# Query products as fp32 in two column halves, and a new order, in the attention stage of a gated mix

## The chip, the cores and the metric

The kernel runs on one core of a Trainium2 chip. The metric is the time of one execution on the device in microseconds (us); smaller is better. Beside the times there is a trace of one profiled execution, in which TensorE is called PE, VectorE DVE, ScalarE ACT, GpSimd POOL and SyncE SP.

## The reference

For one sequence of S = 2048 tokens with D = 576 features, the result is a mix of a linear attention and a gated MLP, by a gate of its own for each token:

```python
g = sigmoid((x * gate_w).sum(-1, keepdims=True))
# a: 32 heads of 18 features
pq, pk = q @ w_phi, k @ w_phi                         # per head
phi_q = concat([softmax(pq), softmax(-pq)])           # 36 features a head
phi_k = concat([softmax(pk), softmax(-pk)])
kv, z = phi_k^T @ v, phi_k.sum over tokens            # per head: 36 x 18, 36
a = ((phi_q @ kv) / (phi_q @ z + 1e-6)) @ wo
b = (max(x @ W_gate, 0) * (x @ W_up)) @ W_down        # F = 4608
return g * a + (1 - g) * b
```

## The kernel before

Everything is fp32. Most products are made on PE in fp32r, with every operand split into a high part (a rounded copy, made by ACT) and a low part (the difference, made by DVE), so that one product is three matmuls: high by high, high by low, low by high. Some small products and all transposes take fp32 operands as they are.

The work falls into three stages.

**Projections and state.** Token tiles of 128 are projected into keys, values and queries (`project`, L179). `key_steps` (L268) and `query_steps` (L344) make the two softmaxes of a tile on DVE, ACT and POOL. `kv_step` (L408) adds a tile into the state: eleven fp32 matmuls, one for each group of 54 value columns with its ones column, the odd groups into rows 64 and up of the same PSUM bank, the even ones into the rows from 0. `turn` (L365) transposes the query features of a tile, in three parts (`QN`: groups 0 to 3, 4 to 7, 8 to 10), to [108 features, 11 groups, 128 tokens]. Tiles before `FIRST` = 12 are stored in DRAM (`eT`); the last four are split right away into operands `phh`, `phl` (L374). The last steps of this stage (L585 on) are written out by hand, with an order for PE kept by `in_order`; the other engines are ordered by a scheduler.

**Attention output.** The state is transposed (`kv_turn`) and masked into per-group weights `kvm` (`kv_blocks`, L505), split into `kvh` and `kvl`. The tokens are then handled in four blocks of 512, in the order 3, 0, 1, 2 (`BLOCKS`). For each block:

- `sums` (L531): for each of six row tiles (`ORDER` = 4, 5, 3, 2, 1, 0) two groups are multiplied into one PSUM bank, three fp32r matmuls for a group, 108 rows deep and 114 columns wide: 108 numerators and six denominators. That is 33 matmuls a block.
- `sums_out` (L540): ACT evicts the 114 rows into `R[:, i]` or a tile `og`; SP copies the denominator rows into a tile `dn` of [128, 128] by a small DMA, and POOL's queue fills the rows 108 to 127 of `R` from row tile 4 (L550) and the fifth row tile from row tiles 4 and 5 (L553, L554).
- `invert` (L689): DVE takes the reciprocal of `dn`, multiplies by the gates, which stand transposed in `gT`, spreads them over four masked copies (`rd`, 128x512) with `cmask`, and the result is split (`rdh`, `rdl`).
- `divide` (L705): for each of the five row tiles two matmuls by `spread` bring the inverted denominators to the rows of `R`; DVE multiplies, ACT and DVE split into `oh` and `ol`.
- `project_out` (L732) and `rows_out` (L756): the output projection by `wo`, 65 matmuls a block, goes over k (the row tile of the input) and for each k over five PSUM banks, one for each row tile m of the output; the five are evicted at the end and stored in `att` in DRAM.

For blocks 0, 1 and 2 of the sequence the query features come back from `eT` in `fetch` (L424) and are split by `prepare_high` and `prepare_low` (L433, L438). `out_weights` (L442) splits `wo` early and stores it in DRAM; `load_out_weights` (L675) loads it back before the output stage. The order of PE in this stage (L915 to L1034) works out as: the sums of the next block between the divisions of the one before, the projection of a block behind the sums of the block after it. `operand_ahead`, `in_place`, `unit` and `load_w` between them are preparations of the third stage.

**Main loop.** The MLP goes over 72 units of 7 products (`step`, L1315), each of 7 matmuls, with the down products between; the attention is added from `att`, in tiles `ac`. Here the order of all engines is fixed by `in_order` (L1473).

Of the kernel before, what the change touches and what calls it, by code (L numbers as in the profile page):

```python
# [15 lines left out]
P = 128  # L16
# [10 lines left out]
NJ = -(-H // HG)  # L27
QH = 3
QG = QH * DH
QK = 2 * QG  # L30
QM = G + 2 * QH
# [51 lines left out]
def gated_mix_kernel(  # L83
# [14 lines left out]
    cmask_d: bass.AP,  # L98
# [15 lines left out]
    keep = ctx.enter_context(tc.tile_pool(name="keep", bufs=1))  # L114
    dram = ctx.enter_context(tc.tile_pool(name="dram", bufs=1, space=bass.MemoryType.DRAM))
# [8 lines left out]
    wohd = dram.tile([P, 5, 5, P], F32, name="wohd")  # L124
    wold = dram.tile([P, 4, 5, P], F32, name="wold")
    sprd = dram.tile([P, 5, P], F32, name="sprd")
# [4 lines left out]
    A, A2, AR = ExitStack(), ExitStack(), ExitStack()  # L131
# [7 lines left out]
    raw = AR.enter_context(tc.tile_pool(name="raw", bufs=4))  # L139
# [108 lines left out]
    pp = A.enter_context(tc.tile_pool(name="pp", bufs=2, space=PSUM, reuse_waits="tile"))  # L248
    pv1 = A.enter_context(tc.tile_pool(name="pv1", bufs=1, space=PSUM, reuse_waits="tile"))
# [53 lines left out]
    def half_gates(hf):  # L303

        c = slice(hf * NT // 2, (hf + 1) * NT // 2)
        nc.vector.tensor_scalar_add(gs[:, c], gs[:, c], 1.0)
        nc.vector.reciprocal(gs[:, c], gs[:, c])
        nc.vector.tensor_scalar(out=ng[:, c], in0=gs[:, c], scalar1=-1.0, scalar2=1.0, op0=MULT, op1=ADD)
# [8 lines left out]
    def on_all_rows(ps, dst, tb):  # L317

        for i in range(4):
            t = 4 * tb + i  # L320
            nc.tensor.transpose(ps[:, i * P:(i + 1) * P], rs[:, t:t + 1].to_broadcast([P, P]), ident)
        nc.scalar.activation(dst, ps, AF.Copy)
# [42 lines left out]
    def turn(t, b, ps=None):  # L365
# [36 lines left out]
    ps_kv = A.enter_context(tc.tile_pool(name="ps_kv", bufs=1, space=PSUM, reuse_waits="tile"))  # L402
# [16 lines left out]
    def operands(tb):  # L419
        PH[tb] = [[ph.tile([QK, len(n), TB], F32R, name=f"ph{a}{n.start}") for a in "hl"] for n in QN]  # L420

    ER = {}

    def fetch(t):  # L424
        ER[t] = er.tile([QK, NQ, P], F32, name="er")
        nc.sync.dma_start(ER[t].rearrange("p g t -> p (g t)"), eT[t * QK:(t + 1) * QK])

    def part(tb, i, p):
        if tb not in PH:
            operands(tb)  # L430
        return *(a[:, :, i * P:(i + 1) * P] for a in PH[tb][p]), ER[4 * tb + i][:, QN[p].start:QN[p].stop]

    def prepare_high(tb, i, p):  # L433

        h, l, r = part(tb, i, p)
        nc.scalar.activation(h, r, AF.Copy)

    def prepare_low(tb, i, p):  # L438
        h, l, r = part(tb, i, p)
        tt(out=l, in0=r, in1=h.bitcast(F32), op=SUB)  # L440

    def out_weights(m):  # L442

        w = raw.tile([P, 5, P], F32, name="wor", tag="raw")
        nc.sync.dma_start(w, wo[m] if m < 5 else spread_d)
        o = raw.tile([P, 2, 5, P], F32R, name="woo", tag="raw")
        nc.scalar.activation(o[:, 0], w, AF.Copy)
        if m < 4:
            tt(out=o[:, 1], in0=w, in1=o[:, 0].bitcast(F32), op=SUB)
            nc.sync.dma_start(wold[:, m], o[:, 1].bitcast(F32))  # L450
        elif m == 4:
            tt(out=o[:, 0, :, 64:], in0=w[:, :, 64:], in1=o[:, 0, :, 64:].bitcast(F32), op=SUB)
        nc.sync.dma_start(wohd[:, m] if m < 5 else sprd, o[:, 0].bitcast(F32))

    xw = AR.enter_context(tc.tile_pool(name="xw", bufs=4, **R_))
    first_half = iter(())
    for t in range(2, NT - 2):
# [10 lines left out]
        if t == 12:  # L468
# [6 lines left out]
            ph = RS.enter_context(tc.tile_pool(name="ph", bufs=1, **R_))  # L475
            kt = kt_p.tile([P, NJ, QK], F32, name="kt")
            gsx = kt_p.tile([P, NTB, H, 4], F32, name="gsx")
            operands(BLOCKS[0])
        keys(t)
# [10 lines left out]
        if t in (2, 3, 4, 5, 7, 8):  # L490
            out_weights((2, 3, 4, 5, 7, 8).index(t))
# [13 lines left out]
    def kv_blocks(q):  # L505

        n, ps = min(4, NQ - 4 * q), PKV[q]
        for p in range(2):
            gs_ = slice(4 * q + p, 4 * q + n, 2)
            ng = len(range(p, n, 2))  # L510
            r = 64 * p
            if q == 2 and p == 0:
                tt(out=kvm[:, 8, 0:QG], in0=ps[:, 0, 1:1 + QG], in1=mask, op=MULT)
                tt(out=kvm[:, 10, DH:QG], in0=ps[:, 1, 1:1 + QG - DH], in1=mask[:, DH:], op=MULT)
            else:
                tt(out=kvm[:, gs_, p * QG:(p + 1) * QG], in0=ps[:, 0:ng, r + 1:r + 1 + QG],
                   in1=mask[:, None, :].to_broadcast([QK, ng, QG]), op=MULT)
            nc.vector.scalar_tensor_tensor(
                out=kvm[:, gs_, G + 3 * p:G + 3 * p + 3], in0=ps[:, 0:ng, r:r + 1].to_broadcast([QK, ng, 3]),
                scalar=eps, in1=hm[:, None, :].to_broadcast([QK, ng, 3]), op0=ADD, op1=MULT)  # L520
        nc.scalar.activation(kvh[:, 4 * q:4 * q + n, :QM], kvm[:, 4 * q:4 * q + n], AF.Copy)

    def kv_low(q):
        n = min(4, NQ - 4 * q)
        tt(out=kvl[:, 4 * q:4 * q + n, :QM], in0=kvm[:, 4 * q:4 * q + n],
           in1=kvh[:, 4 * q:4 * q + n, :QM].bitcast(F32), op=SUB)

    DN, RW, OG, PS = {}, {}, {}, {}
    ORDER = (4, 5, 3, 2, 1, 0)

    def sums(tb, i, ps):  # L531

        PS[tb, i] = ps = ps[:QM]
        parts, pairs = PH[BLOCKS[tb]], []
# [5 lines left out]
    def sums_out(tb, i):  # L540
        if i == ORDER[0]:
            pool = ob if tb % 2 else rb
            DN[tb], RW[tb] = (pool.tile(shape, F32, name=name, bufs=1) for name, shape in (("dn", [P, P]), ("R", [P, 5, TB])))
        dn, R = DN[tb], RW[tb]
        og = OG[i] = R[:QM, i] if i < 4 else rb.tile([P, TB], F32, name="og")[:QM]
        nc.scalar.activation(og, PS.pop((tb, i)), AF.Copy)
        d0, dl = (G, HG) if i < NJ - 1 else (G + 1, 2)
        nc.sync.dma_start(dn[4 * HG * i:4 * (HG * i + dl)], og[d0:d0 + dl])
        if i < 4:
            nc.gpsimd.dma_start(R[G:, i], OG[4][20 * i:20 * i + 20])  # L550
        elif i == 5:
            for r in (0, 64):
                nc.gpsimd.dma_start(R[r:r + 28, 4], OG[4][80:G])  # L553
                nc.gpsimd.dma_start(R[r + 28:r + 64, 4], OG[5][DH:QG])  # L554
# [30 lines left out]
    with in_order(tc, nc, nc.tensor):  # L585
# [3 lines left out]
        run(key_steps, t, (T_(t - 2, 1),), V_(t - 1, 0), F_, K_(t - 2), T_(t - 2, 0))  # L589
        run(query_steps, t, (V_(t - 1, 1),))  # L590
        run(query_steps, FIRST - 2, (V_(t, 0),), V_(t, 1), F_, K_(t - 1), T_(t - 1, 2), K_(t))
        kv_out()
        A2.close()
        kb = RS.enter_context(tc.tile_pool(name="kb", bufs=1, **R_))
        rb = RS.enter_context(tc.tile_pool(name="rb", bufs=2, **R_))
        er = RS.enter_context(tc.tile_pool(name="er", bufs=4, **R_))
        table = kb.tile([QK, 64], F32, name="table")[:, :QG + 4]
# [1028 lines left out]
```

## Time and profile before

| | us |
|---|---|
| median of 3 runs | 1635.37 |
| lowest and highest run | 1634.16, 1635.42 |
| profiled execution | 1633.52 |
| its span in the trace | 1631.7 |
| first state step of the last tile ends, main loop begins on PE | 251.6, 377.9 |

The profiled execution is 1.8 us longer than its span, and 1.9 us below the median of the runs. Its mean granted clock of PE is .991 of full speed. In the profile a line such as "L1204 DVE TENSOR_TENSOR ac<-pd,ac 128x512 f32<-128x512 f32 x238 | 163.9, 689 | 148.0 <-PE pd L1189 147.9" reads: line 1204, on DVE, writes ac from pd and ac, 238 times; 163.9 us busy in all, 689 ns each; DVE stood idle for 148.0 us just before them, 147.9 of it until a product pd of PE at line 1189. L177 is the helper `accumulate`, L371 a transpose in `turn`, L412 the state step and L753 the output projection.

### The profile page before, as it was taken

The numbers are of one execution on the slowest core, as the hardware profiler recorded it, in microseconds if no ns is written. First come the engines' busy times: TensorE is split into PE (matmuls) and PEld (weight loads), VectorE is DVE, ScalarE is ACT, GpSimd is POOL, SyncE is SP. The second block draws the span as 40 slices with busy tenths as digits, with TensorE's granted clock in tenths as the row PEclk, the third lists the DMA queues.
The fourth block names the chain that finished last, engine by engine and source line by source line (L and its number), as shares of the span: only waits on it lengthen the run. The fifth ranks groups of instructions, "written<-read, shape, count | busy, mean of one in ns | idle before, by whom it ended". The sixth has DMA issues, their size and how long they took to land.

```text
span 1631.7 us, 20454 instructions
## 1 busy us (share of the span) xinstructions
PE 1591.5 (98%) x7887; PEld 1341.4 (82%) x7887; DVE 1230.6 (75%) x1907; ACT 579.2 (35%) x960; POOL 181.7 (11%) x266
## 2 busy tenths in 40 slices
PE   9998997998999999999999999999999999999998
PEld 8898996776888888888888887788888888888887
DVE  4998687758777787887777777667777777777777
ACT  4344335655332432332332334232322223222331
POOL 0128212220000000000000002111111111111110
PEclk9999999999999999999999999999999999999999
DMA  8244107466766657556545534553434434343442
GB/s 268 82 158 168 59 17 235 160 216 238 272 222 218 232 197 256 207 194 231 225 171 204 200 123 130 208 198 131 173 138 154 172 130 182 128 177 149 151 160 73
DMA packets 64861, 285.84 MB, mean 175 GB/s; under 512 B 7290, under 2 KB 16890, under 8 KB 55804
## 3 DMA queue, kind: packets, MB, share of 16 engines
q1 hardware_dynamic: 61932, 278.24, 47.1%
q0 software_dynamic: 2256, 5.25, 1.0%
q8 instruction: 62, 1.02, 0.3%
q10 hardware_dynamic: 576, 1.05, 0.2%
q14 instruction: 35, 0.29, 0.1%
HBM read 173.00 MB, written 109.54 MB: 173 GB/s over the span
## 4 chain that ended last, share of the span: by engine, by line
PE 85%; DVE 5%; DMA 4%; ACT 3%; issue 2%; POOL 1%; SPq 0%; POOLq 0%; DVEq 0%; ACTq 0%
PE cx L1126 27%; PE ca L1126 13%; PE pd L1166 12%; PE pd L1189 10%; PE cy L1126 7%; PE kv L177 2%; PE pq L177 2%; PE pm L1166 2%; PE pm L1189 2%; PE pw L753 2%; PE pk L177 2%; PE pv L239 1%; PE po L177 1%; DVE sm L206 1%; PE ptr L371 1%
## 5 line engine op out<-in xcount | busy, mean ns | idle before, releaser
L1233 ACT ACTIVATE hh<-g 128x512 fp32r<-128x512 f32 x195 | 119.9, 624 | 455.0 <-DVE g L1283 285.7
L1204 DVE TENSOR_TENSOR ac<-pd,ac 128x512 f32<-128x512 f32 x238 | 163.9, 689 | 148.0 <-PE pd L1189 147.9
L1126 PE MATMUL cx<-xo,ws 128*128 128x512 f32 x1008 | 253.7, 391 | 4.3 <-ACT g L1287 4.3
L1126 PE MATMUL cx<-xo,wb 128*128 128x512 f32 x1008 | 250.4, 391 | 4.5 <-DVE u L1408 2.7
L1126 PE MATMUL ca<-xo,ws 128*128 128x512 f32 x1008 | 251.9, 389 | 0.0
L1126 PEld LDWEIGHTS cx<-xo,wb 128*128 128x128 f32 x1008 | 188.6, 188 | 46.4 <-DVE u L1408 3.5
L1126 PEld LDWEIGHTS cx<-xo,ws 128*128 128x128 f32 x1008 | 189.9, 189 | 44.8 <-ACT g L1287 5.4
L1126 PEld LDWEIGHTS ca<-xo,ws 128*128 128x128 f32 x1008 | 189.3, 188 | 39.3
L1166 PE MATMUL pd<-hh,wd 128*128 128x512 f32 x576 | 200.7, 389 | 0.0
L1189 PE MATMUL pd<-hh,wd 128*128 128x512 f32 x476 | 185.6, 390 | 0.0
L1172 DVE TENSOR_TENSOR ac<-pd,ac 128x512 f32<-128x512 f32 x144 | 99.1, 688 | 105.9 <-PE pd L1166 103.3
L1238 DVE TENSOR_TENSOR hl<-g,hh 128x512 fp32r<-128x512 f32 x195 | 136.2, 699 | 1.9 <-ACT hh L1233 0.2
L1287 ACT ACTIVATE g<-cx 128x512 f32<-128x512 f32 x144 | 84.7, 588 | 127.4 <-PE cx L1126 127.3
L1166 PEld LDWEIGHTS pd<-hh,wd 128*128 128x128 f32 x576 | 108.1, 188 | 22.5
L1126 PE MATMUL cy<-xo,wb 128*128 128x512 f32 x504 | 126.0, 389 | 0.0
L1089 ACT ACTIVATE wd<-wdr 128x384 fp32r<-128x384 f32 (+1 forms) x106 | 62.3, 606 | 156.5 <-DMA wdr<-wd 156.5
L1166 PE MATMUL pd<-hl,wd 128*128 128x512 f32 x288 | 112.2, 389 | 1.0 <-ACT xo L815 1.0
L1126 PEld LDWEIGHTS cy<-xo,wb 128*128 128x128 f32 x504 | 94.7, 188 | 19.7
L1189 PEld LDWEIGHTS pd<-hh,wd 128*128 128x128 f32 x476 | 89.6, 188 | 18.7
L1189 PE MATMUL pd<-hl,wd 128*128 128x512 f32 x238 | 92.8, 390 | 0.0
L799 POOL TENSOR_TENSOR xo<-xr,xo 32x512 fp32r<-32x512 f32 x5 | 8.2, 1654 | 635.6 <-DVE xo L799 628.0
L1092 DVE TENSOR_TENSOR wd<-wdr,wd 128x384 fp32r<-128x384 f32 (+1 forms) x106 | 69.5, 670 | 6.2 <-ACT wd L1089 6.2
(241 smaller groups left out, 2708.2 us busy)
## 6 DMA issues: line engine op xcount, KB each, us to landing
wsd<-ws SPq DMA_DIRECT2D x34, 1280.0 KB
ws<-wsd SPq DMA_DIRECT2D x34, 1280.0 KB
wbd<-wb SPq DMA_DIRECT2D x34, 960.0 KB
wb<-wbd SPq DMA_DIRECT2D x34, 960.0 KB
wr<-wgu SPq DMA_DIRECT2D x36, 768.0 KB
wdr<-wd SPq DMA_DIRECT2D x36, 576.0 KB
eT<-et SPq DMA_DIRECT2D x12, 594.0 KB
er<-eT SPq DMA_DIRECT2D x12, 594.0 KB
```

What stands on the lines that cost most here:

```text
L177: nc.tensor.matmul(ps, w, m, start=i == 0, stop=i == len(pairs) - 1)
L753: nc.tensor.matmul(ps, w, v, start=len(done) == 1, stop=len(done) == (14 if m < 4 else 9), skip_group_check=True)
L1089: nc.scalar.activation(o[:, 0], a, AF.Copy)
L1092: tt(out=o[:, 1], in0=a, in1=o[:, 0].bitcast(F32), op=SUB)
L1126: nc.tensor.matmul(ps, w, v, start=first and m == 0, stop=m == len(pairs) - 1, skip_group_check=True)
L1166: nc.tensor.matmul(ps, w, v, start=k == 0 and (i < 2 or first), stop=k == len(mms) - 1 and (i < 2 or last), skip_group_check=True)
L1172: tt(out=a, in0=ps, in1=a, op=ADD)
L1189: mm = lambda ps, w, v, a, z: nc.tensor.matmul(ps, w, v, start=a, stop=z, skip_group_check=True)
L1204: tt(out=a, in0=ps, in1=a, op=ADD)
L1233: nc.scalar.activation(h, src, AF.Copy)
L1238: tt(out=l, in0=src, in1=h.bitcast(F32), op=SUB)
L1287: nc.scalar.activation(a, ps, AF.Copy)
```

## The change

1. The products of `sums` take fp32 operands as they are: no `kvh`, `kvl`, `phh`, `phl`. The weights of a group have 64 columns (`QM` = 64): the even group of a row tile goes to PSUM rows 0 to 63, the odd one to 64 to 127. A block has 11 matmuls. `fetch` loads straight into the operand tile; in `turn` one ACT copy stands in place of the split.
2. The denominators of a block are 32 rows of 512 (`dn`), gate rows come by four transposes to 32 columns a block (`rows_of`), and the inverted rows, high over low, are one operand of 64 rows: `divide` has one matmul for a row tile.
3. `project_out` goes over the row tiles m of the output, with all k for one m, in two PSUM banks in turn, and evicts each at once. The split `wo` is loaded from DRAM into the pool `raw` before the last token tiles (at t = 12 of the first loop) and stays there.
4. Blocks: in `project_out(b, m)` stand the sums of block b + 2 and the division of block b + 1. One query tile (10) goes behind the last state step. SP's and POOL's queues follow the program's order too. `fetch` of the third block comes behind the sums of the second.
5. The PSUM pools `pp`, `pv1` and `ps_kv` are kept until the attention is done (`AP`), in place of new pools `pw` and `pb`; `raw` is kept to the end and takes the tiles `ac` of the main loop. `load_w(0)` and what follows it stand behind the last division of block 3, in `project_out(2, 1)`.

The diff, cut to its core:

```diff
+GAP = 10
-QM = G + 2 * QH
+QM = 64
...
-            h, l = (a[:, :, t % 4 * P:(t % 4 + 1) * P] for a in PH[t // 4][b])
-            split(h, l, ps[:, :len(gg)])
+            nc.scalar.activation(PH[t // 4][:, t % 4, gg.start:gg.stop], ps[:, :len(gg)], AF.Copy)
...
+def fetch(tb):
+        operands(tb)
+        for i in range(4):
+            t = 4 * tb + i
+            nc.sync.dma_start(PH[tb][:, i].rearrange("p g t -> p (g t)"), eT[t * QK:(t + 1) * QK])
...
+    def sums(b, i, ps):
+        if i == ORDER[0]:
+            DN[b] = rb.tile([H, TB], F32, name="dn", bufs=1)
+            RW[b] = rb.tile([P, 5, TB], F32, name="R")
+            OG4[b] = rb.tile([P, TB], F32, name="og")
+        dn, R = DN[b], RW[b]
+        n = P if i < NJ - 1 else QM
         for g in range(2 * i, min(2 * i + 2, NQ)):
-            (h, l), o = parts[g // 4], g % 4
-            pairs += [(kvh[:, g, :QM], h[:, o]), (kvh[:, g, :QM], l[:, o]), (kvl[:, g, :QM], h[:, o])]
-        accumulate(ps, pairs)
+            nc.tensor.matmul(ps[g % 2 * 64:g % 2 * 64 + QM], kvm[:, g], PH[BLOCKS[b]][:, :, g], start=True, stop=True)
+        og = (OG4[b] if i == 4 else R[:, i if i < 4 else 4])[:n]
+        nc.scalar.activation(og, ps[:n], AF.Copy)
+        if i < NJ - 1:
+            nc.sync.dma_start(dn[HG * i:HG * i + HG], og[64 - QH:64 + QH])
+        else:
+            nc.sync.dma_start(dn[HG * i:], og[:2])
         if i < 4:
+            nc.gpsimd.dma_start(R[QG:QG + 2 * GAP, i], OG4[b][i // 2 * 74 + i % 2 * 20:][:20])
         elif i == 5:
+            for r, c in ((0, 40), (14, 114)):
+                nc.gpsimd.dma_start(R[r:r + 14, 4], OG4[b][c:c + 14])
...
+    def invert(b):
+        dn = DN.pop(b)
+        ps = kv_bank(0)
+        rows_of(ps, gs, BLOCKS[b], H)
+        nc.vector.reciprocal(dn, dn)
+        tt(out=dn, in0=ps[:H], in1=dn, op=MULT)
+        rd = RD[b] = rb.tile([2 * H, TB], F32R, name="rd", bufs=1)
+        nc.scalar.activation(rd[:H], dn, AF.Copy)
+        tt(out=rd[H:], in0=dn, in1=rd[:H].bitcast(F32), op=SUB)
+
+    def divide(b, k):
+        R = RW[b]
+        n = P if k < 4 else 64
...
+        nc.tensor.matmul(ps[:n], spread[:, k, :n], RD[b], start=True, stop=True)
+        r = R[:n, k]
+        tt(out=r, in0=ps[:n], in1=r, op=MULT)
+        nc.scalar.activation(oh[:n, k], r, AF.Copy)
+        tt(out=ol[:, k] if k < 4 else oh[64:, k], in0=r, in1=oh[:n, k].bitcast(F32), op=SUB)
...
+        last = query_steps(FIRST - 2, middle)
...
+        for i, ps in zip(ORDER, (kv_bank(0), kv_bank(1), two[:, 0], two[:, 1], kv_bank(0), kv_bank(1))):
+            sums(0, i, ps)
...
+        final = query_steps(FIRST - 1, middle)
+        next(final)
+        whole(last)
+        turn(FIRST - 2, 0)
+        turn2(FIRST - 2, 1)
+        turn(FIRST - 2, 2)
+        two = pp.tile([P, 2, TB], F32, name="po", tag="pp")
+        sums(1, ORDER[0], two[:, 0])
+        sums(1, ORDER[1], two[:, 1])
+        next(final)
+        next(final)
+        invert(0)
+        for n in (2, 4):
+            two = pp.tile([P, 2, TB], F32, name="po", tag="pp")
+            divide(0, 6 - n)
+            sums(1, ORDER[n], two[:, 0])
+            divide(0, 5 - n)
+            sums(1, ORDER[n + 1], two[:, 1])
+        fetch(BLOCKS[2])
+        divide(0, 0)
+        whole(final)
+        turn(FIRST - 1, 0)
...
+    def project_out(b, m):
+        ps = kv_bank(2) if m % 2 else pv1.tile([P, TB], F32, name="pw", tag="pv1")
+        oh, ol = OW[b]
+        pairs = []
+        for k in range(4, -1, -1):
+            wh, wl = WOUT[m, k]
+            pairs.append((wh, oh[:, k]))
+            if k < 4:
+                pairs.append((wh, ol[:, k]))
+            if m < 4:
+                pairs.append((wl, oh[:, k]))
+        accumulate(ps, pairs)
...
+        fetch(BLOCKS[3])
+        for b in range(2):
+            for m in range(5):
+                project_out(b, m)
+                if m < 3:
+                    two = pp.tile([P, 2, TB], F32, name="po", tag="pp")
+                    for n in range(2):
+                        sums(b + 2, ORDER[2 * m + n], two[:, n])
+                if m == 0:
+                    invert(b + 1)
+                else:
+                    divide(b + 1, 5 - m)
+                if b == 0 and m in (3, 4):
+                    root_rows(m - 1)
+                if m == 4:
+                    divide(b + 1, 0)
+                    whole((x0, x1)[b])
+        for m in range(5):
+            project_out(2, m)
+            if m == 0:
+                invert(3)
+                divide(3, 4)
+                divide(3, 3)
+            if m == 1:
+                for k in (2, 1, 0):
+                    divide(3, k)
                 RS.close()
...
-    ac = ctx.enter_context(tc.tile_pool(name="ac", bufs=1, **CB))
+    sums_of = [raw.tile([P, 3, TB], F32, name="ac", tag="raw") for _ in range(4)]
```

More of the change, by code (lines that the diff above doesn't have):

```diff
@@ L419, in operands @@
     def operands(tb):
[L420 to L440, printed above, removed]
+        PH[tb] = PP[BLOCKS.index(tb) % 2].tile([QK, 4, NQ, P], F32, name="ph")
+    def fetch(tb):
[3 more added lines that the diff above has]
+            nc.sync.dma_start(PH[tb][:, i].rearrange("p g t -> p (g t)"), eT[t * QK:(t + 1) * QK])
     def out_weights(m):
         w = raw.tile([P, 5, P], F32, name="wor", tag="raw")
-        nc.sync.dma_start(w, wo[m] if m < 5 else spread_d)
+        nc.sync.dma_start(w, wo[m])
         o = raw.tile([P, 2, 5, P], F32R, name="woo", tag="raw")
@@ L540, in sums_out @@
[L540 to L548, printed above, removed]
+                out=kvm[:, gs_, d:d + QH], in0=ps[:, 0:ng, r:r + 1].to_broadcast([QK, ng, QH]),
@@ L647, in gated_mix_kernel @@
-        PH.pop(b0)
-        pg = pp.tile([P, 2, TB], F32, name="pgt", tag="pp")[:, 0]
-        for tb in range(NTB):
-            nc.tensor.transpose(pg[:, tb * P:(tb + 1) * P], gsx[:, tb].rearrange("p h c -> p (h c)"), ident)
-        nc.scalar.activation(gT.rearrange("p b t -> p (b t)"), pg, AF.Copy)
-        turn(FIRST - 1, 0)
-        two = pp.tile([P, 2, TB], F32, name="ptr", tag="pp")[:QK].rearrange("p b (g t) -> p b g t", g=4)
-        turn(FIRST - 1, 1, two[:, 0])
-        turn(FIRST - 1, 2, two[:, 1])
```

375 lines of the change are left out of this document (107 added, 268 removed).

## Prediction

> **What bounds the kernel now.** The page first, then busy time by windows, then the waits of TensorE, then the chain. The page says that TensorE (PE) is the bound as a whole:
>
> ```profile
> span 1631.7 us, 20454 instructions
> PE 1591.5 (98%) x7887; PEld 1341.4 (82%) x7887; DVE 1230.6 (75%) x1907; ACT 579.2 (35%) x960; POOL 181.7 (11%) x266
> er<-eT SPq DMA_DIRECT2D x12, 594.0 KB
> ```
>
> PE is idle for 1631.7 − 1591.5 = 40.2 us in all. The change leaves the order of the main loop alone, so it works only on the attention stage, from about 245 us to the loop's first product at 377.94 us (row below), and on the entry of the loop behind it. What counts is when PE begins unit 0 of the loop; a microsecond there is one at the end, since PE is busy from there on. The windows (length, PE, PEld, DVE, ACT, POOL, granted clock, DMA share, GB/s) show where the stage is not PE's:
>
> ```profile
> 250.00:260.00 10.00, 8.56 (x79) 7.73 (x79) 7.66 (x25) 6.38 (x12) 1.17 (x1) 1.00 0.83 279
> 270.00:280.00 10.00, 6.88 (x36) 4.93 (x34) 7.90 (x13) 6.21 (x13) 3.52 (x7) 1.00 0.78 245
> 280.00:290.00 10.00, 4.11 (x10) 3.15 (x11) 2.54 (x4) 2.99 (x7) 1.38 (x3) 0.56 0.39 129
> 290.00:300.00 10.00, 10.00 (x42) 8.00 (x41) 8.83 (x15) 8.03 (x17) 1.67 (x4) 0.93 0.68 227
> ```
>
> At 280 us PE idles, and afterwards works at about half clock. The waits of PE from 255 to 400 us name the reasons (engine and line that waits, what it waits for, total, times, longest):
>
> ```profile
> PE pd L177 <- ACT og L546: 7.6, 1, 7.6
> PE cx L1126 <- ACT g L1287: 2.7, 1, 2.7
> PE pw L753 <- DVE o L765: 1.8, 1, 1.8
> PE cx L1126 <- DVE u L1408: 1.6, 1, 1.6
> PE ptr L371 <- DVE phl L151: 1.4, 2, 1.1
> PE ptr L371 <- DVE et L382: 1.4, 2, 0.7
> PE ptr L371 <- ACT et L380: 0.7, 1, 0.7
> ```
>
> The chain of waits tells what is behind the 7.6 us, and gives PE's pace in the sums (start, length, what):
>
> ```profile
> 271.42 5.79 DMA dn<-R
> 277.74 7.33 DMA R<-og
> 285.24 0.61 ACT og L546
> 285.89 1.22 PE pd L177 x2
> 312.47 2.77 PE po L177 x12
> 385.02 5.42 DMA wdr<-wd
> ```
>
> ACT could not evict the next og, because a small transfer out of the old og took 7.33 us and had itself waited for a denominator transfer of 5.79 us. So block 0 is bound by small transfers in crowded queues, and everything later by PE.
>
> **The change, part by part.** Sums. Twelve fp32r products take 2.77 us, .231 each, so a block's 33 take 7.6 us. The new block has 11 fp32 products in column halves, which no row shows at 512 columns; the nearest is the state's step L412, eleven fp32 products in the same two halves, 108 columns wide (start, length, engine, line, what):
>
> ```profile
> 249.89 0.54 PE L371 MATMUL ptr<-ident,e 128*108 128x128 f32 x3
> 250.36 1.32 PE L412 MATMUL kv<-e,vt 128*55 128x108 f32 x22
> 251.61 0.40 PE L177 MATMUL pq<-wq_h,xh 128*128 128x288 f32 x1
> 251.85 0.29 PE L177 MATMUL pq<-wq_l,xh 128*128 128x288 f32 x1
> 251.98 0.29 PE L177 MATMUL pq<-wq_h,xl 128*128 128x288 f32 x1
> 253.56 0.60 PE L371 MATMUL ptr<-ident,e 128*108 128x128 f32 x4
> 254.00 0.82 PE L503 MATMUL kv<-ident,kt 128*108 128x128 f32 x6
> ```
>
> ```profile
> 377.94 1.75 PE L1126 MATMUL cx<-xo,wb 128*128 128x512 f32 x7
> ```
>
> Four transposes take 254.00 − 253.56 = .44 us, .11 each. The three ahead of the step take .47, .14 more than .33: entering costs .14. The first product behind it takes .24 and the second .13: leaving costs .11. Together .25 us a visit. Start to start the step takes 1.25 us; less .14 that is 1.11 for eleven products, .101 each. At the pace of the .11 transposes (.86 ns a column and record, two records a product) one alone would take .186, so the halves run beside each other. Widened by 512/108 the block takes 11 × .101 × 4.74 = 5.3 us, or 8.8 to 9.7 if the halves did not overlap. I take 5.3, which is 2.3 less a block and 9.2 in all.
>
> The Trainium skill's page "TensorEngine Tiling (Array Packing)", Key Properties, says that a change of tiling mode drains TensorE, which speaks against this change; by that rule each visit has a price, and the trace agrees with .25 us.
>
> Switches. Sums are visited 12 times (once in block 0, five times in block 1, between divisions, three in each of the others): 3.0 us. Twenty spread products of 64 rows and four sets of 32-column transposes stand between full-size products; no row has these tiles, so 0 to .25 each; I take half, 3.0. Together +6.0, with ends 3.0 and 9.0.
>
> Division. One spread product in place of two: 20 × .231 = −4.6. Gate rows: 16 transposes of 32 columns instead of 4: 12 × .11 = +1.3.
>
> The same page, Gotcha 2, rules out transpose mode for fp32 beside column tiling; by it these transposes might cost two records, 16 × .11 = 1.8 us more. No run here shows it.
>
> Work of PE altogether: −9.2 + 6.0 − 4.6 + 1.3 = −6.5 us.
>
> Stalls that go. The 7.6 us: of og only row tile 4 is left, so its two buffers reach back two blocks instead of one. The 1.4 + 1.4 + .7 at the turns and the 1.8 at L753 (one eviction per row tile, beside the next tile's products) go too: −12.9. The half clock goes as well: the windows grant .56 from 280 to 290 and .93 from 290 to 300 us, so it ends at about 291.4; from 285.9 to there 5.5 us of work took twice its time: −2.7. What is late next is DVE and the queues:
>
> ```profile
> L440 DVE TENSOR_TENSOR phl<-er,phh 108x512 fp32r<-108x512 f32 x24 | 15.6, 682 | 0.3
> L711 DVE TENSOR_TENSOR R<-pd,R 128x512 f32<-128x512 f32 x20 | 13.4, 688 | 16.9 <-PE pd L177 15.1 <-DMA R<-og 1.7
> L726 DVE TENSOR_TENSOR ol<-R,oh 128x512 fp32r<-128x512 f32 x16 | 10.9, 689 | 5.5 <-ACT oh L713 5.1
> L206 DVE TENSOR_REDUCE sm<-e 128x64 f32<-128x1152 f32 x6 | 8.1, 1353 | 3.5 <-ACT e L203 3.5
> L692 DVE RECIPROCAL dn<-dn 128x128 f32<-128x128 f32 x4 | 3.8, 950 | 3.0 <-DMA dn<-R 3.0
> L201 DVE TENSOR_TENSOR e<-pq,mx 128x576 f32<-128x576 f32 x4 | 3.0, 747 | 0.0
> L307 DVE RECIPROCAL gates<-gates 128x8 f32<-128x8 f32 x1 | 0.2, 195 | 0.0
> ```
>
> ```profile
> L713 ACT ACTIVATE oh<-R 128x512 fp32r<-128x512 f32 x20 | 12.2, 627 | 13.4 <-DVE R L711 12.6 <-ACT phh L436 0.8
> L436 ACT ACTIVATE phh<-er 108x512 fp32r<-108x512 f32 x24 | 14.0, 631 | 0.0
> ```
>
> ```profile
> L550 POOL DMA_DIRECT2D R<-og x16 | 8.1, 509 | 24.4 <-DMA dn<-R 22.6 <-ACT phh L436 1.8
> ```
>
> The splits L436 and L440 leave ACT and DVE, 14.0 and 15.6 us in these rows. Against that, the reciprocal goes from 128 elements a row to 512. It rises by (950 − 195)/120 = 6.3 ns an element, so 512 take .95 + 384 × .0063 = 3.4 us instead of .95, if 32 rows are no quicker than 128. Behind the landing of the last denominators (5.79 us in the crowded queue) the new chain is reciprocal 3.4, product .69, copy .63, difference .69: 5.4 us of DVE and ACT, 2.5 more than with a reciprocal of .95.
>
> New stalls, followed through the new order of each engine, with block 0's sums done at 260 us:
> - query tile 10, now behind the last state step, is turned after a softmax chain (sm 1.35, exponential, scaling on GpSimd): 1.5.
> - dn of block 0 lands at 263.0, reciprocal to 266.4; ahead of rd DVE does the softmax of query tile 11 (four passes of .75 and sm, 4.3 us), so the first division is at 274.7, while block 1's first sums and tile 10's turns have ended at 270: 4.7.
> - five divisions, one a ring of spread, product .69, copy .63, difference .69 with an eviction between, bound by DVE and ACT: 9.3 us beside 6.3 of PE's work: 3.0. Then tile 11's turns wait until its scaling on POOL, now in program order behind R's copies (L550 waits 22.6 us for dn), is done, and the first project_out for the last division: 3.0.
> - fetch of block 2 is issued by SP behind the dn of block 1, at about 282.7. Four transfers of 594 KB, 2.43 MB, take 10.7 us at 227 GB/s (290 to 300 us) and about 1.8 to begin, so they land at 295.2; its sums stand on PE at 291.2: 4.0. At 279 GB/s it would be 2.0.
> - in block 1's projection the reciprocal for block 2 (3.4) stands on DVE between a division's product and its difference: 4.0. In block 2's, where the others are shorter: 1.8, and 3.7 ahead of the first division of block 3, since DVE and ACT do an operand of the loop first.
>
> Sum 1.5 + 4.7 + 6.0 + 4.0 + 4.0 + 1.8 + 3.7 = 25.7 us. All are estimates by hand and their lower end is nothing for the fetch and the reciprocal (−15); above, a stall that stretches another could add 6.
>
> Clock. After 7.6 idle us the old trace has some 10 us at half clock. The stalls of 4 to 6 us at 270 to 290 are near that: 0 to 3.4 us lost, I take 2.0.
>
> Entry. load_w and the operands start a little later in the order but the raw pool stays, and the wait of 2.7 and 1.6 shrink because evictions ahead of it are done one by one: −1.6, between −3 and +2 (the 5.42 us of wdr follow SP's last store of att).
>
> Sum: −6.5 − 12.9 − 2.7 + 25.7 + 2.0 − 1.6 = +4.0 us. The profiled execution, 1633.5 us with 1.8 around its span, becomes 1637.5. The median shown is 1635.4, 1.9 above it, so the forecast is **1639.4**.
>
> **Rivals.**
> - The lead is kept (faster). Place: the reciprocal and the fetch. If 32 rows are quicker, or the order leaves room, so that the reciprocal costs under 1.5 us of path, the 4.7, 4.0 and 3.7 shrink by some 2 each, and the fetch at 279 GB/s or more by 2 to 4: −9, so −5: 1630. For it: DVE and ACT lose 15 us each, and the old order has a single large stall. Against: 6.3 ns an element by two rows. It decides from about −4 us of stalls.
> - The halves do not overlap over 512 columns: 3.5 to 4.4 more a block, 14 to 18, of which the stalls hide some 4, so 12 on top of the +4.0: 1651.4. Against: the step at L412.
> - About the same: the clock stays full and fetch and one DVE stall are missed, −4: 1635.5.
> - The change is not two blocks ahead where it matters: the fetch of block 2 comes behind dn. That is in the forecast already.
>
> **How the numbers follow.** Forecast .50 (own range 1636 to 1645; .12 of it under +0.2%), faster rival .27, no overlap .12, same .11. A measurement of this kernel tells about 0.2%, 3.3 us. Faster .27; same .12 + .11 = .23; slower .38 + .12 = .50. The range takes in the faster rival with 3 us beyond it and the slow one to 1655: 1627 to 1655.
>
> **What would show it.** Step by step: sums of a block 5.3 us (wrong at 9); .25 us at the switches; DVE RECIPROCAL 32x512 near 3.4 us; PE's waits at 270 to 290 us on DVE, one at about 291 on the fetch, then on DVE in blocks 1 to 3; unit 0 at about 383.5 us instead of 377.9 (the sum without the entry's −1.6). Wrong if PE starts unit 0 before 377, if no wait on a reciprocal shows, or if the half clock lasts over 10 us.

## The result, and the profile after

The changed kernel takes 1654.48 us (median of 4 runs, 1653.22 to 1659.41) against 1635.39 of the kernel before on the same chips. The ratio is 1.0124, with a 95% interval from 1.0102 to 1.0145: 19 us slower. The forecast was 4 us slower; the time lies at the upper edge of its range, in the place of the slow rival, but for another reason than that rival's. The profiled execution took 1653.61 us, with this at the head of its page:

```profile
span 1651.8 us, 20195 instructions
PE 1600.2 (97%) x7835; PEld 1323.3 (80%) x7835; DVE 1210.2 (73%) x1853; ACT 562.5 (34%) x918; POOL 177.8 (11%) x259
PEclk9999997899999999999999999999999999999999
```

Fewer instructions on every engine, less busy time on DVE, ACT and POOL, and a longer span. The third line has a 7 and an 8 in it: the granted clock of PE fell in the slices from 248 to 330 us (41.3 us each). The windows bound the stage by its own events: the end of the last state step (251.61 before, 246.64 after), the first product of the main loop (377.94, 397.43) and the first down product (410.99, 431.48). First the kernel before (columns as in the prediction; the eighth number is the clock):

```profile
251.61:377.94 126.33, 113.38 (x520) 90.98 (x520) 89.75 (x154) 75.06 (x132) 27.31 (x49) 0.96 0.58 194
377.94:410.99 33.05, 27.67 (x113) 21.85 (x112) 26.55 (x37) 17.04 (x24) 0.00 (x0) 0.95 0.87 321
```

Then the changed kernel:

```profile
246.64:397.43 150.79, 125.40 (x496) 76.77 (x496) 74.78 (x111) 59.63 (x92) 25.03 (x43) 0.86 0.40 144
397.43:431.48 34.05, 29.48 (x114) 22.79 (x112) 28.04 (x40) 16.88 (x24) 0.00 (x0) 0.90 0.78 287
```

The stage is 24.5 us longer, of which 5.0 are given back because it begins earlier (one query tile less in front of it). The entry of the loop is 1.0 longer and the rest .4 shorter: 24.5 − 5.0 + 1.0 − .4 = 20.1, the difference of the two spans. Inside the stage PE's idle time rose from 12.95 to 25.39 us, and its busy time from 113.4 to 125.4 although it has 24 records fewer. The reason for the second is the clock. One stretch at half clock, and six windows of 3.41 us in and around it, show it in the changed kernel (3.41 us because every stretch at half clock in this stage is that long or a multiple of it):

```profile
267.70:298.42 30.72, 22.39 (x51) 8.37 (x48) 16.81 (x26) 11.59 (x18) 4.27 (x7) 0.50 0.34 114
```

```profile
264.28:267.70 3.42, 1.83 (x14) 1.33 (x15) 3.38 (x4) 0.00 (x0) 0.99 (x1) 1.00 0.05 12
267.70:271.11 3.41, 2.72 (x6) 0.29 (x2) 3.10 (x5) 0.60 (x1) 0.00 (x0) 0.50 0.48 167
277.93:281.35 3.42, 3.42 (x8) 0.86 (x6) 1.38 (x2) 1.70 (x4) 1.05 (x2) 0.50 0.09 20
281.35:284.76 3.41, 3.41 (x8) 0.87 (x9) 1.64 (x3) 1.55 (x3) 1.04 (x2) 0.50 0.05 16
295.00:298.41 3.41, 3.41 (x9) 2.64 (x8) 0.00 (x0) 0.00 (x0) 0.00 (x0) 0.50 0.86 309
298.41:301.80 3.39, 2.63 (x11) 1.14 (x10) 0.00 (x0) 1.19 (x2) 0.60 (x1) 1.00 0.99 413
```

Behind a window with 1.83 of 3.42 us busy the clock is at half for 30.7 us. The 22.39 us of work in there would have taken half of that: 11.2 us lost. Two shorter stretches, at 325.7 and 366.7 us, lose 4.1 more the same way: 15.3 in all. The kernel before has one stretch and loses 2.8 (third line):

```profile
325.72:332.55 6.83, 4.88 (x12) 3.82 (x13) 5.44 (x7) 2.01 (x3) 0.55 (x1) 0.50 0.19 58
366.68:370.10 3.42, 3.42 (x9) 2.67 (x9) 1.56 (x3) 0.85 (x2) 0.00 (x0) 0.50 0.00 0
281.21:291.45 10.24, 5.56 (x13) 4.26 (x14) 3.43 (x6) 3.89 (x8) 2.04 (x4) 0.50 0.32 104
```

So the 24.5 us are 12.4 of idle time and 12.6 of clock, less .5 of work. Note the windows at 278 and 281 us: PE is busy without a gap (as the profile models the ends of products) and yet does not get its clock back.

The longest waits of PE from 245 to 420 us. The one at L1019 was there before, and so was one for `o` at the projection, 1.8 us once; it is now 5.0 in three:

```profile
PE kv L579 <- DVE rd L568: 6.4, 2, 3.5
PE ptr L374 <- POOL e L209: 5.2, 2, 4.2
PE pw L175 <- DVE o L719: 5.0, 3, 2.7
PE po L542 <- ACT R L544: 3.8, 5, 1.0
PE cx L1019 <- DVE u L1301: 2.9, 1, 2.9
PE po L542 <- ACT og L544: 2.1, 3, 0.8
```

And the parts themselves, as PE's timeline has them at full clock: a row tile of sums with two groups, one with a single group, the gate transposes, and a spread product with the product behind it:

```profile
299.73 1.08 PE L542 MATMUL po<-ph,kvm 108*64 108x512 f32 x4
301.56 1.07 PE L542 MATMUL po<-ph,kvm 108*64 108x512 f32 x2 [0.76 <-ACT og L544]
302.56 0.61 PE L320 MATMUL kv<-ident,gates 128*32 128x128 f32 x4
302.93 0.94 PE L175 MATMUL kv<-oh,wo 128*128 128x512 f32 x3
309.11 0.45 PE L579 MATMUL kv<-rd,spread 64*64 64x512 f32 x1
309.49 0.96 PE L175 MATMUL pw<-oh,wo 128*128 128x512 f32 x3
```

Two groups take no longer than one: the halves run beside each other at 512 columns too, and the slow rival is out. The reciprocal is as worked out (name and shapes as before, times, busy and mean, idle before):

```profile
L564 DVE RECIPROCAL dn<-dn 32x512 f32<-32x512 f32 x4 | 13.3, 3336 | 4.6 <-DMA dn<-R 4.6
```

### The profile page after: what moved, and what is told of

Its sections match the earlier page's. It is cut to its first block, busy times and chain, and to the rows that moved or that the text cites. A ratio compares the mean times of both kernels' runs of the same rounds, so it can differ in the third digit from the quotient of the medians.

```text
span 1651.8 us, 20195 instructions
## 1 busy us (share of the span) xinstructions
PE 1600.2 (97%) x7835; PEld 1323.3 (80%) x7835; DVE 1210.2 (73%) x1853; ACT 562.5 (34%) x918; POOL 177.8 (11%) x259
## 4 chain that ended last, share of the span: by engine, by line
PE 87%; DVE 5%; DMA 2%; ACT 2%; issue 2%; POOL 1%; SPq 0%; ACTq 0%; DVEq 0%; POOLq 0%
PE cx L1019 27%; PE ca L1019 13%; PE pd L1059 12%; PE pd L1082 10%; PE cy L1019 7%; PE kv L175 3%; PE pw L175 2%; PE pq L175 2%; PE pm L1059 2%; PE pm L1082 2%; PE pk L175 2%; PE po L542 2%; DVE sm L204 1%; PE ptr L374 1%; PE pv L237 1%
## 5 line engine op out<-in xcount | busy, mean ns | idle before, releaser
L1019 PE MATMUL cx<-xo,wb 128*128 128x512 f32 x1008 | 252.2, 393 | 4.5 <-DVE u L1301 3.5
L1019 PE MATMUL cx<-xo,ws 128*128 128x512 f32 x1008 | 252.4, 390 | 3.4 <-ACT g L1180 3.4
L1019 PE MATMUL ca<-xo,ws 128*128 128x512 f32 x1008 | 252.0, 389 | 0.6 <-DMA ws<-wsd 0.6
L1019 PEld LDWEIGHTS cx<-xo,wb 128*128 128x128 f32 x1008 | 189.9, 190 | 46.8 <-DVE u L1301 4.3
L1019 PEld LDWEIGHTS cx<-xo,ws 128*128 128x128 f32 x1008 | 188.9, 188 | 44.2 <-ACT g L1180 5.1
L1019 PEld LDWEIGHTS ca<-xo,ws 128*128 128x128 f32 x1008 | 189.3, 188 | 40.4 <-issue 1.0
L1019 PE MATMUL cy<-xo,wb 128*128 128x512 f32 x504 | 125.9, 389 | 0.0
L1019 PEld LDWEIGHTS cy<-xo,wb 128*128 128x128 f32 x504 | 94.6, 188 | 19.6
```

The costliest lines, as they stand in the source:

```text
L1019: nc.tensor.matmul(ps, w, v, start=first and m == 0, stop=m == len(pairs) - 1, skip_group_check=True)
```

## The experiments

Two theories stood against each other. **Clock**: the missing 15 us are PE at half clock, a cost of its own. **Queues**: the stretch is bound by DVE, ACT, POOL and small transfers, and the clock falls because PE waits. Times are medians beside the kernel before on the same chip; ratios are to that kernel. The changed kernel has 1.0124. Gains below are differences of medians, between runs on several chips; the ratios put those over the changed kernel up to 3 us higher. Losses by the clock are read from one profiled execution each.

**e1_fill.** Products that nobody reads, at the waits:

```diff
+    def fill(ps, n):
+        for _ in range(n):
+            nc.tensor.matmul(ps, wq_h[:, 0, :P], X[NTB - 1][0][:, 0], start=True, stop=True)
...
+        fill(ps, 4)        # 3, 16 and 2 ahead of later turns, 12 ahead of divide(0, 4)
         turn(FIRST - 2, 0)
```

> The changed kernel with PE kept busy at its waits between 264 and 295 us: 37 products of 128x512 that nobody reads, of operands that are there already, put into PSUM banks ahead of the transposes, the first division and the first projection that wait there; they are overwritten. Theory 'clock': the 15 us that the forecast lacks are PE at half clock, 267.7 to 298.4 us in the changed kernel's trace, entered because of idle time and not left because of it. Filled, the stretch stays at 1.00, the 22.4 us of work in it take 11.2 less; the chain through DVE takes some of that back, so the kernel gets 6 to 11 us faster (1643 to 1648). Theory 'queues': the stretch is bound by DVE, ACT, POOL and small transfers and the clock is only a symptom: within 2 us of the changed kernel, whatever the clock.

Measured: 1648.61 us, 1.0083 (1.0068 to 1.0098), 5.9 under the changed kernel. The stretch keeps its clock:

```profile
264.30:290.10 25.80, 21.36 (x94) 11.36 (x92) 20.52 (x29) 11.14 (x18) 5.52 (x9) 1.00 0.27 89
```

The first projection starts at 290.1 instead of 294.5 us. The loss by the clock in the stage, read as above, falls from 15.3 to 4.9 us and the idle time from 25.4 to 21.0, but the 37 fillers take 9.8 us of PE themselves: the stage is 4.6 us shorter (146.2). Another 2.3 come at the entry of the loop, which has no half clock in this execution (31.7 us instead of 34.05). The gain is at the lower end of what theory "clock" said and well above what "queues" said. A wait of 1.2 us for the fetch is new.

**e2_scale_early.** `whole(final)` moved from behind `divide(0, 0)` to ahead of `invert(0)`.

> The changed kernel with the last query tile's normalisation (DVE reciprocal and product, scaling on POOL) put ahead of invert(0) instead of behind the last division of block 0. In the changed kernel PE waits 4.2 us for that scaling at 291.2 us, and the scaling stands on POOL behind the copies of R. Theory 'queues': the 4.2 go, and the stretch behind them starts 3 to 4 us sooner. Theory 'clock': the 4.2 go and, as the stretch has fewer idle windows, the half clock ends sooner too: 4 to 9 us faster (1645 to 1650).

Measured: 1655.16 us, 1.0121 (1.0105 to 1.0136): nothing gained, both theories missed. The wait of 4.2 us for POOL is gone, and another stands in its place:

```profile
PE po L542 <- DMA ph<-eT: 8.0, 1, 8.0
```

The projection starts 6 us earlier, at 288.7, but the transfers of the third block are issued behind block 1's denominators at 286.2 and PE's sums wait for them until 300.1.

**e3_short_recip.** `nc.vector.reciprocal(dn[:, :8], dn[:, :8])` in place of the whole rows.

> The changed kernel with each block's reciprocal over 8 of the 512 columns only (the other 504 columns keep the denominator itself, so the output is not the reference's). By the forecast the reciprocal costs 3.4 us each, of which 2.9, 4.0, 1.8 and 3.7 us of stalls depended in part. Theory 'reciprocal': each of three stalls shrinks by 2 to 3, and with them the clock's losses at 325 and 366 us (2.4 and 1.7): 8 to 12 us faster. Theory 'clock' without it: the first wait alone shrinks and PE stays at half clock: 2 to 4 us faster.

Measured: 1654.33 us, 1.0106 (1.0088 to 1.0124): .15 us under the changed kernel by the medians, although four reciprocals of 3.34 us became four of .19 us. By the ratios it is some 3 us faster, with overlapping intervals. The 8 to 12 us were missed; the 2 to 4 are not excluded. So by itself the reciprocal is worth little in this kernel. (It is worth more later, below.)

**e4_full_tiles.** The spread and its operand get 128 rows, 64 of them zeros, and the gate transposes 128 columns:

```diff
-        rows_of(ps, gs, BLOCKS[b], H)
+        rows_of(ps, gs, BLOCKS[b], P)
...
-        nc.tensor.matmul(ps[:n], spread[:, k, :n], RD[b], start=True, stop=True)
+        nc.tensor.matmul(ps, spread[:, k], RD[b], start=True, stop=True)
```

> The changed kernel with the spread products and the transposes of the gate rows on the full 128x128 array: the operand of the inverted denominators gets 64 rows of zeros, its weights too, and the gate transposes fill 128 columns. Theory 'drains': the spread of 64 rows takes .72 us a time at half clock where 512 columns would be .43, and it is these breaks that keep the clock down between 276 and 287 us though PE waits for nothing there: the clock comes back one or more windows sooner, 3 to 8 us faster. Theory 'waits alone': the spread keeps its time, within 2 us of the changed kernel.

Measured: 1653.04 us, 1.0108 (1.0092 to 1.0123), within the scatter. At half clock the spread takes the same on the full array (.77 us from its start to the next sums, 278.50 to 279.27, against .76 in the changed kernel), and the clock is at half from 275.9 to 299.8 us, with PE busy throughout for the first three windows of it. So the 64-row tiles are not what keeps the clock down. In this run's groups:

```profile
L580 PE MATMUL kv<-rd,spread 128*128 128x512 f32 x20 | 10.4, 534 | 7.9 <-DVE rd L569 6.8 <-DVE R L582 1.1
```

against 8.5 + 2.0 us for the twenty of the changed kernel. The busy time hides a difference at full clock, though: behind a full-size product the spread takes .43 us to the next start in the changed kernel (319.50 to 319.93 us) and .22 here (319.86 to 320.08).

**e5_fill_fetch.** e1_fill, and `fetch(BLOCKS[2])` right behind block 0's sums.

> The changed kernel with the products of e1_fill that nobody reads, and with the fetch of the third block issued right behind block 0's sums instead of behind block 1's. In e1_fill the transfers land at 294.6 us and PE, which would have begun the third block's sums at 293.6, waits. Theory 'what is next behind the clock is the fetch': those waits go, the clock stays full in that window too, 2 to 4 us under e1_fill (1645 to 1647). Rival 'early transfers slow the small ones': the denominators of blocks 0 and 1 land behind 2.4 MB and the divisions start later: the same as e1_fill or slower.

Measured: 1650.64 us, 1.0085 (1.0067 to 1.0103), level with e1_fill. The wait for the fetch is gone; one of 3.9 us for DVE at the divisions of block 1, at 323.3 us, came for it, and the half clock behind that. The fetch was next in line, and DVE right behind it.

**e6_sep_banks.** A tile of its own for each row tile of sums:

```diff
-                    two = pp.tile([P, 2, TB], F32, name="po", tag="pp")
+                    two = [pp.tile([P, 2, TB], F32, name="po", tag="pp")[:, 0] for _ in range(2)]
                     for n in range(2):
-                        sums(b + 2, ORDER[2 * m + n], two[:, n])
+                        sums(b + 2, ORDER[2 * m + n], two[n])
```

> The changed kernel with a PSUM tile of its own for each row tile of sums, in place of the two halves of one tile of two banks. In the changed kernel's trace the second sums of each pair wait .7 to 1.0 us until ACT has evicted the first ones (3.8 and 2.1 us in all), though they write another bank. Theory 'shared tile': the wait is for the tile as a whole, and goes: 5.9 us less idle, and 3 to 7 us off the time, less where the next wait takes it back. Rival 'ACT': the wait is for ACT itself and stays: within 2 us.

Measured: 1649.26 us, 1.0077 (1.0062 to 1.0092), 5.2 under the changed kernel. The waits of L542 for `R` are gone and .7 for `og` is left: PE had waited for the tile as a whole while ACT read the other bank of it.

**e7_all.** e5_fill_fetch and e6_sep_banks together.

> e5_fill_fetch and e6_sep_banks together. If the causes named so far (half clock 15 us, fetch 3, shared tile 6) are separate and make up the loss, the kernel comes to 1638 to 1642, within 7 us of the kernel before. If the stretch is really bound by the chain through DVE and ACT, it stays at 1645 or above.

Measured: 1642.55 us, 1.0040 (1.0026 to 1.0054), 12 under the changed kernel. What waits now is seen best on DVE, as PE waits for the projection's bank until 320.2 us:

```profile
315.69 0.68 DVE L586 TENSOR_TENSOR R<-kv,R 128x512 f32<-128x512 f32 x1
316.29 3.33 DVE L564 RECIPROCAL dn<-dn 32x512 f32<-32x512 f32 x1
319.55 0.62 DVE L730 TENSOR_TENSOR o<-b,pw 64x512 f32<-64x512 f32 x1
320.10 0.67 DVE L588 TENSOR_TENSOR ol<-R,oh 128x512 fp32r<-128x512 f32 x1
```

The eviction of block 0's last row tile and a difference of block 1's division stand behind the next block's reciprocal: the stall that the prediction put at 4.0 us.

**e10_all_short.** e7_all with the short reciprocals of e3_short_recip.

> e7_all with the reciprocals over 8 of 512 columns only (the other columns keep the denominator itself, so the output is not the reference's). In the changed kernel alone this gained nothing that could be told (e3_short_recip), while PE was bound by the half clock. In e7_all the wait of 4.7 us at 320 us ends with an addition on DVE that stands behind a reciprocal of 3.3 us. Theory 'the reciprocal is next in line': that wait falls to some 1.5 and the half clock behind it goes (2 us): 4 to 7 us under e7_all. Rival 'not on the path': within 2 us of e7_all.

Measured: 1634.79 us, .9998 (.9989 to 1.0007): level with the kernel before, 7.8 under e7_all. The same edit that gained .15 us in e3_short_recip gains 7.8 (6.9 by the ratios) where the clock, the fetch and the shared tile no longer cover it.

**e9_all_x1_late.** e7_all, `whole(x1)` behind `divide(3, 3)`.

> e7_all, and the main loop's second operand (1.2 and .7 us of DVE, 1.5 of ACT) made behind the first two divisions of block 3 instead of ahead of them. In e7_all PE waits 3.5 us for rd of block 3, and 1.9 of it is DVE at that operand. Theory 'order on DVE': the wait falls to about 1.6 and the half clock behind it (3.4 us long, 1.7 lost) with it: 2 to 4 us under e7_all. Rival: the operand is then late for the loop's second product or stands before the last divisions: no gain.

Measured: 1640.54 us, 1.0036 (1.0022 to 1.0050), 2.0 under e7_all, with overlapping intervals: no gain is shown. The wait at block 3's first division fell from 3.5 to 2.1 us, but 1.3 came back at its last.

**e12_fill_between.** Plain products not at the waits but between the sums:

```diff
+            fill(two[:, 0], 4)
             sums(1, ORDER[n], two[:, 0])
...
+            fill(two[:, 1], 4)
             sums(1, ORDER[n + 1], two[:, 1])
```

> The changed kernel with four products of 128x512 that nobody reads ahead of each of the four sums between block 0's divisions, and nothing at the waits: PE enters the stretch at half clock as in the changed kernel. There, the clock stayed at half from 277.9 to 284.8 us though PE waited for nothing; in e1_fill the same sums and spreads ran at full clock throughout. Theory 'the kind of work counts': sums in column halves and spreads hold a full clock but do not bring it back, plain products do: the clock comes back inside the stretch, before 288 us, and the fillers (16 x .23 to .43 us) cost less than they bring: 0 to 4 us faster. Rival 'the time counts': the clock stays at half to the projection as before, and the kernel is 4 to 7 us slower.

Measured: 1658.66 us, 1.0145 (1.0131 to 1.0160), not faster, rather 4 slower. The clock does come back inside the stretch, after one full window:

```profile
277.80:281.20 3.40, 3.40 (x9) 1.47 (x9) 2.27 (x9) 0.63 (x1) 0.54 (x2) 0.50 0.02 5
281.20:284.60 3.40, 3.13 (x13) 1.05 (x9) 1.38 (x2) 1.23 (x2) 0.51 (x1) 1.00 0.09 21
```

So for the clock the kind of work counts, and for the time it does not help: in the profiled execution the fillers cost 5 us, the waits grew by 3, and the 7 us of clock saved went into them. Two things weaken this run. Its half clock began only at 277.8 us, behind a window with .11 us busy, and not at 267.7 as expected. And the profiled execution is the fastest of four and has the highest clock over the whole run (.990; the others .984 to .986), so the others lost more by it.

**e13_waits_gone** and **e14_waits_gone_fill.** Fewer waits by order: the edits of e6, the early fetch, e2 and e9, and the reciprocal in four pieces, those of blocks 2 and 3 in the projection before; e14 with the first 19 fillers of e1_fill.

```diff
+    def inverse(b, j):
+        d = DN[b][:, j * P:(j + 1) * P]
+        nc.vector.reciprocal(d, d)
...
                 if m in (3, 4):
+                    inverse(b + 2, 2 * m - 6)
+                    inverse(b + 2, 2 * m - 5)
```

> The changed kernel without any product that nobody reads, but with the waits found so far taken away: a PSUM tile for each row tile of sums, the third block's fetch behind block 0's sums, the last query tile's scaling ahead of invert(0), the second operand of the main loop behind the first divisions of block 3, and the reciprocals in four pieces of 128 columns, those of the last two blocks ahead of time in the projection before. The full output is computed. Theory 'the half clock follows from the waits': with them gone it falls from 15 us of loss to under 5 by itself, and the kernel comes to 1636 to 1642. Rival 'the kind of work in the stretch keeps the clock down': PE still enters at half clock near 265 to 278 us and stays there to the first projection, with 8 us of loss or more: 1643 to 1648.

> e13_waits_gone with the fillers of e1_fill ahead of tile 10's transposes and of the first division (19 products). If the clock is a cost of its own beside the waits: 3 us or more under e13_waits_gone, 1634 to 1638, level with the kernel before. If the half clock only takes up time that the chain through DVE, POOL and the small transfers needs anyway: within 2 us of e13_waits_gone.

Measured: 1640.21 us, 1.0027 (1.0016 to 1.0038), and 1637.60 us, 1.0019 (1.0006 to 1.0033). e13_waits_gone gains 14.3 of the 19 us without a filler. Its stage:

```profile
246.54:383.86 137.32, 120.06 (x497) 76.09 (x496) 75.53 (x123) 59.34 (x92) 24.98 (x43) 0.91 0.47 158
```

Idle time is 17.3 us (137.3 − 120.1) and the loss by the clock still 11.1 (three stretches, 23.9 us long, of which 22.3 busy). So the rival was right about the clock and the theory about the time. The waits are not all gone: PE still waits 4.4 us for `rd` at the first division, and the half clock begins right behind that. What the waits do not explain is how long it lasts. PE is busy in all four windows of that stretch, of which these are the first and the last:

```profile
274.20:277.61 3.41, 3.41 (x8) 0.88 (x10) 1.65 (x4) 1.23 (x2) 0.53 (x2) 0.50 0.09 35
284.44:287.86 3.42, 3.36 (x14) 2.26 (x12) 1.73 (x3) 2.19 (x5) 0.67 (x2) 0.50 0.07 16
```

The fillers gain 2.6 more, with overlapping intervals: 5.3 us less lost by the clock and 2.8 less idle, against 5.0 more work.

**e8_before_og.** The other way round: the kernel before with `bufs=4` for `og`.

> The kernel before with four buffers for og instead of two, nothing else. The forecast took the wait of 7.6 us at 285.9 us and the half clock behind it (2.7) to come from the old og's copy. Theory: both go and 5 to 10 us are gained (1626 to 1631), some of it given back where PE then waits for the inverted denominators. Rival: the copies of R are late in the queue anyway and the division would wait for them: within 2 us of the kernel before.

Measured: 1630.82 us, .9970 (.9959 to .9980): 4.7 us faster, the fastest of all that were run. The waits of PE at the first division are 2.1 and 1.0 us instead of 7.6:

```profile
PE pw L753 <- DVE o L765: 2.4, 1, 2.4
PE pd L177 <- ACT rdh L700: 2.1, 1, 2.1
PE pd L177 <- DVE rdl L702: 1.0, 1, 1.0
```

**e11_before_og_fill.** That, with eight fillers at each of its two waits.

> e8_before_og (the kernel before with four og buffers) with eight products that nobody reads ahead of the first division of block 0 and eight ahead of the last block's projection, where PE waits 3.1 and 2.4 us and then works 6.8 and 3.4 us at half clock. Theory 'clock': those 4.7 us of loss go, less what the fillers take beyond the waits: 2 to 4 us under e8_before_og (1627 to 1629). Rival: the waits grow by as much: the same.

Measured: 1632.75 us, .9988 (.9978 to .9997): not faster than e8_before_og. In the profiled execution, one of the fastest of twelve (1629.87), the clock is at 1.00 through the stage and PE's busy time the same (115.5 against 115.4): the fillers took what the clock gave.

## Why the prediction was wrong, point by point

- **Work of PE, −6.5.** Nearly right. Busy time less the clock's loss is 113.4 − 2.8 = 110.6 before and 125.4 − 15.3 = 110.1 after; with the query tile that moved in (28 products at .13 and 11 transposes at .11, some 4.9 us) the saving is 5.4. A row tile of sums takes about 1.08 us, so the six of a block take 6.5, against 5.6 to 6.6 forecast (5.3 and one to five switches of .25). The gate transposes take .37 us for four, not twice that.
- **Stalls that go, −12.9.** Right for 10.1 of it: the 7.6 are gone, and of the 3.5 at the turns 1.0 is left. The 1.8 at the projection did not go: waits for the same addition on DVE are 5.0 in three, 2.7 of it the reciprocals' stall below. e8_before_og shows that the og buffers were behind the 7.6 us: with four of them 3.1 are left at that division.
- **New stalls, 25.7.** The sum is right (25.4 idle) by luck; the list is not. Tile 10's turns took 1.6 (1.5 forecast), the first division 2.9 (4.7), the reciprocals' stall 2.7 (4.0), block 3's first division 3.5 (3.7). The fetch took 0 instead of 4.0, because PE came 8.5 us later than the list had it (299.7 instead of 291.2). Block 0's five divisions waited for nothing behind the first (3.0 forecast), as PE's own work there ran at half clock. In their place stand 5.9 us that the list did not have: the second sums of each pair waiting for ACT to read the first ones' bank of the same tile.
- **Clock, "0 to 3.4 us lost, I take 2.0".** This step failed. 15.3 us were lost, 13.3 more than forecast, and that is most of the 16 us between forecast (1637.5) and profiled execution (1653.6); the entry is 2.6 of them and PE's work 1. The forecast asked only how long the waits are, and took some 4 us of work at half clock (2.0 lost). What it did not see: the window that triggers it need not be even half idle (1.83 of 3.42 us busy), and the work behind it, sums in halves and spreads, does not end it, even with PE busy throughout. The first is no rule: in e2_scale_early and e4_full_tiles windows at the same place with 1.81 and 1.82 us busy kept the clock, and it fell two windows later, behind the wait for the first division.
- **Entry, −1.6.** Wrong by 2.6: 34.05 against 33.05 us. The waits at the third and fifth products shrank from 2.7 to 1.1 us, as expected, but the first one for DVE at L1301 grew from 1.6 to 2.9, and two windows of half clock stand behind it (3.1 us lost, where the kernel before loses 1.5 in one). The idle time is .8 less than before: here too it was the clock.
- **Rivals.** No overlap of the halves: refuted, though it named nearly the measured time. The reciprocal as the place of decision: not in the changed kernel (e3_short_recip), but once the other three are away it is worth 7.8 us (e10_all_short).

The causes overlap, so they do not add up one by one. In the order tried: fillers −5.9, or separate tiles −5.2; with both and the early fetch −12; with the short reciprocals −19.7, level with the kernel before. How much of the 19 us belongs to the clock alone stays open: fillers gain 2.6 us with fewer waits (e14_waits_gone_fill against e13_waits_gone) and 5.9 with all of them (e1_fill), but they cost work themselves, and the loss read from the trace is 15.3. What keeps e13_waits_gone 4.7 us behind the kernel before is in its stage: 4.3 us more idle time and 8.3 more lost by the clock, against 1.7 less work and a stage that begins 5.1 us earlier.

## What to carry to other kernels

Where a forecast finds new waits, ask of each window of 3.41 us (the step of the half clock in these traces) how busy PE is in it, and whether the work behind it is of a kind that brought the clock back in a trace. Here the loss by the clock grew as much as the waits themselves, 12.6 against 12.4 us, but filling the waits gained 5.9 us where it took 10.4 of that loss away (e1_fill): the fillers take PE's time too, and other engines then hold PE back. Removing one of several overlapping waits may show nothing (e2, e3); test it again where the others are away. And two banks in one PSUM tile made the writer of one wait for the reader of the other here (5.9 us in all, .7 with a tile for each).

## What the runs showed of the hardware

- The half clock ended after a window full of plain 128x512 products (295.0 to 298.4 us in the changed kernel), after one with 2.1 us of them (277.8 to 281.2 in e12_fill_between), and in e13_waits_gone after one with 2.7 us of 128x128 transposes of fp32 (284.4 to 287.9). It did not end after two windows full of fp32 products of 64 columns with spreads between (277.9 to 284.8 in the changed kernel), nor after three (274.2 to 284.4 in e13_waits_gone). In e1_fill the same sums and spreads, entered at full clock, kept it. The Trainium skill's page "TensorE: Matmul & The Clock Gate", section "What's actually happening", has PE back at full clock after one busy window of some 3.4 us; by the windows at 277.93 and 281.35 busy alone is not enough here. The 64 rows of the spread are not the reason (e4_full_tiles). Whether the operand type, the 64 columns or the breaks between tile shapes decide was not tried apart.
- A reciprocal costs by the elements of a row and not by the rows: 3.34 us for 32x512, .95 for 128x128, which has as many elements in all.
- A spread product of 64 rows stands .43 us ahead of the next product at full clock, behind a full-size product (319.50 to 319.93), and one of 128 rows .22 (319.86 to 320.08 in e4_full_tiles); their summed busy times for twenty are within .1 us of each other.
